# Loading v's weights from a second queue and reordering the first projection of an attention kernel

## The chip, the cores and the metric

The kernel runs on one core of one Trainium2 chip. The metric is the device time of one execution in microseconds. The kernel before takes 255.29 us, the median of three runs (254.67 to 255.47).

## The reference

Two independent blocks, A and B, each take x (2048 tokens, 640 features) and weights, and their outputs are put side by side. Both split 640 features into 32 heads of 20.

```
qkv = x @ wqkv                        # [2048, 3 * 640]: q, k, v
A: scores = q k^T / sqrt(20), each token sees itself and the 255 before it
   o = softmax(scores) v;  out_A = o @ wo
B: pq, pk = phi(q), phi(k)            # phi(t) = t + 1 above zero, exp(t) below
   o = pq (pk^T v) / (pq . sum pk);   out_B = o @ wo
```

The change touches only the first steps of block A: x of the first 512 tokens, v of those tokens (`x @ wqkv`, last third of the columns) and the preparation of q's weights.

## The kernel before

Tokens go in four blocks of 512. Features are five tiles of 128 (KT = 5), so a product over all features is a chain of five matmuls. After an opening written out by hand, the main loop goes through 76 score tiles of block A (`scores`, L784 the products, L792 the exponential, L807 the masks); between them, `take` fills TensorE with projections of A and B from a plan with due times (`chain`, L276, holds most of those products). The change lies in the opening, and the plan is not touched.

The opening, in the order of the program:

- `load_x_first` loads the first 512 tokens of A in rows to a tile (`phi` in the profile) with `load` (L173), as tokens 0 to 127, 128 to 255, and 256 to 511; `transposes` (L178) turns one block of 128 tokens with five transposes into a PSUM tile (`first`), and two copies bring it to `xA`: VectorE's (L352) for even blocks, ScalarE's (L349) for odd ones.
- v's weights come in three parts by feature tile, `v_parts`: tile 0 (160 KB), tiles 1 and 2 (320 KB), tiles 3 and 4 (320 KB), into `wA` (L968). All are issued by SP: tokens 0 to 127, tokens 128 to 255, first part, tokens 256 to 511, second part, third part, then q's and k's raw weights (L334, 800 KB each, into the tiles that the profile calls `qpad` and `kpad`), a transposing load of the next 512 tokens (L163), and B's first weights and x.
- `warm_up` (L196) gives TensorE products of a zeroed tile that nobody reads: 18 before the transposes of the first block of 128 tokens, and 2 between those of the first and the second block.
- `v_abreast` (L411 the products) computes v for the 512 tokens in eight sums: four blocks of 128 tokens times two halves of the columns. The first four sums are in `dense` tiles of PSUM, the last four in `first` tiles. The loop is over parts outside and sums inside: all eight sums take their products of part one, then of part two, then of part three. After the first four products, the caller's loop puts in the transposes of the third and fourth block. The first four sums are evicted (`v_rows`, by `evac`, L261 ScalarE and L263 VectorE) as each ends; after the last product, the caller's loop calls `regroup` for q, and then the last four sums are evicted.
- `regroup` copies the raw weights of q (then of k) into `wqk`, with each head at a 32-row place: for q, five copies of VectorE (L352), and seven that POOL (L355) and ScalarE (L349) take in turn.
- Then come q's rows (three blocks) and k's rows (two) for the first 512 tokens, by `chain` (L276), and the first score tile. A `dense` tile of PSUM is one of four buffers; q's first row takes the one that the first sum of v had.

Of the kernel before, what the change touches and what calls it, by code (L numbers as in the profile page):

```python
# [9 lines left out]
P = 128  # L10
# [4 lines left out]
F32 = mybir.dt.float32  # L15
# [5 lines left out]
SB = 512  # L21
TPS = SB // P
# [70 lines left out]
def kernel(  # L93
# [10 lines left out]
    nc = tc.nc  # L104
    _, S, D = A_x.shape
    KT = D // P
# [31 lines left out]
    first_ps = opening.enter_context(tc.tile_pool(name="first", bufs=4, space=PSUM))  # L138


    w_sb = {}
# [19 lines left out]
    def load_x(n, s):  # L161
        t = xp.tile([P, KT, SB], BF16, name=f"x{n}")
        nc.sync.dma_start_transpose(out=t[:], in_=xsrc[n][s * SB : (s + 1) * SB, :])  # L163
        return t

    def load_x_first():

        tok = pqp.tile([P, TPS, D], BF16, name="phi")
        src = xsrc["A"][0:SB, :].rearrange("(t p) d -> p t d", p=P)
        t = xp.tile([P, KT, SB], BF16, name="xA")  # L170

        def load(t0, t1):
            nc.sync.dma_start(out=tok[:, t0:t1, :], in_=src[:, t0:t1, :])  # L173

        def transposes(tb):
            ps = first_ps.tile([P, 2 * SB], BF16, name="first")
            for c in range(KT):
                nc.tensor.transpose(  # L178
                    ps[:, c * P : (c + 1) * P], tok[:, tb, c * P : (c + 1) * P], ident[:]
                )  # L180
            dst = t[:, :, tb * P : (tb + 1) * P]
            pv = ps[:, 0:D].rearrange("p (c q) -> p c q", q=P)

            for c in (slice(0, 2), slice(2, KT)):
                (act_copy if tb % 2 else dve_copy)(dst[:, c, :], pv[:, c, :])

        return t, load, transposes

    def warm_up(wait):

        z = op.tile([P, TPS, D], BF16, name="osb")
        nc.vector.memset(z[:, 0, 0:P], 0.0)
        ps = dps.tile([P, SB], F32, name="dense")
        for n in wait:
            for _ in range(n):
                nc.tensor.matmul(  # L196
                    ps[:, 0:P], lhsT=z[:, 0, 0:P], rhs=z[:, 0, 0:P], start=True, stop=True
                )
            yield


# [25 lines left out]
    def flush(before=None):  # L227

        while later and (before is None or later[0][0] <= before):
            later.pop(0)[1]()  # L230
# [9 lines left out]
    def settle(all=True):  # L240
        while posts and (all or posts[0][0] <= begun[0]):
            posts.pop(0)[1]()


    load = {"A": 0, "D": 0}
# [9 lines left out]
    def evac(dst, src, n=SB, to=None):  # L255

        if to is None:
            to = "A" if load["A"] < load["D"] + AHEAD else "D"
        load[to] += n + COPY
        if to == "A":  # L260
            nc.scalar.activation(out=dst, in_=src, func=ACT.Copy)  # L261
        else:
            nc.vector.tensor_copy(out=dst, in_=src)  # L263

    def bank(wide=False):
        flush(begun[0] - 2)
        begun[0] += 1
        settle(False)
        if wide:
            return dps.tile([P, 2 * SB], BF16, name="dense")  # L270
        return dps.tile([P, SB], F32, name="dense")
# [40 lines left out]
    xA, xB = {}, {}  # L312
    q_pad, k_pad, v_tok = {}, {}, {}
# [7 lines left out]
    for c in range(KT):  # L321
        m = EXTRA * c
        while m < EXTRA * (c + 1):
            n = min(EXTRA * (c + 1) - m, DH - m % DH)
# [3 lines left out]
    def load_raw(i):  # L328

        pl, name = ((qp, "qpad"), (kp, "kpad"))[i]  # L330
        t = pl.tile([P, NG, SB], BF16, name=name)
        raw = t.rearrange("p g q -> p (g q)")[:, 0 : KT * D].rearrange("p (k n) -> p k n", n=D)
        wv = A_wqkv.rearrange("(kt p) n -> p kt n", p=P)
        nc.sync.dma_start(out=raw, in_=wv[:, :, i * D : (i + 1) * D])  # L334
        return raw

    def regroup(i, src, heads, extras):

        def four(g):
            return src[:, :, 4 * DH * g : 4 * DH * (g + 1)].rearrange("p k (j d) -> p k j d", d=DH)  # L340

        for c in range(KT):
            dst = wqk[:, i, :, c * P : (c + 1) * P].rearrange("p k (j e) -> p k j e", e=32)
            heads(dst[:, :, :, 0:DH], four(c))
            for _, row, g, d, n in [piece for piece in pieces if piece[0] == c]:
                extras(dst[:, :, :, row : row + n], four(g)[:, :, :, d : d + n])

    def act_copy(dst, src):
        nc.scalar.activation(out=dst, in_=src, func=ACT.Copy)  # L349
# [7 lines left out]
    def in_turn(*fns):  # L357
        n = [0]

        def copy(dst, src):  # L360
            n[0] += 1
            fns[n[0] % len(fns)](dst, src)

        return copy
# [43 lines left out]
    by_tokens = [(tb, i) for tb in range(TPS) for i in range(2)]  # L408

    def v_product(ps, xt, tb, i, kt):  # L410
        nc.tensor.matmul(  # L411
            ps[:, 0 : hh * DH],
            lhsT=xt[:, kt, tb * P : (tb + 1) * P],
            rhs=w_sb["A"][:, kt, i * hh * DH : (i + 1) * hh * DH],
            start=(kt == 0),
            stop=(kt == KT - 1),
        )

    def v_rows(ps, dst, tb, i):
        evac(  # L420
            dst[:, tb, i * hh : (i + 1) * hh, 0:DH],
            ps[:, 0 : hh * DH].rearrange("p (h d) -> p h d", d=DH),
            hh * DH,
        )
# [8 lines left out]
            v_rows(ps, dst, tb, i)  # L433
            yield End(hh * DH)

    def v_abreast(xt, dst, order, parts):

        own = len(order) - 4
        pss = {c: bank() for c in order[:own]}
        for k0, k1 in parts:  # L440
            for c in order:
                if c not in pss:
                    pss[c] = first_ps.tile([P, SB], F32, name="first")
                for kt in range(k0, k1):
                    v_product(pss[c], xt, *c, kt)
                if k1 == KT and c in order[:own]:
                    v_rows(pss[c], dst, *c)
                elif k0 == 0:
                    yield
        yield  # L450
        for c in order[own:]:
            v_rows(pss[c], dst, *c)


# [505 lines left out]

    v_parts = ((0, 1), (1, 3), (3, KT))
    wv = A_wqkv.rearrange("(kt p) n -> p kt n", p=P)
    load_tokens(0, 1)
    load_tokens(1, 2)
    for k0, k1 in v_parts:
        if k0 == 1:
            load_tokens(2, TPS)
        nc.sync.dma_start(out=w_sb["A"][:, k0:k1, :], in_=wv[:, k0:k1, 2 * D : 3 * D])  # L968
    raw = [load_raw(i) for i in range(2)]
    xA[1] = load_x("A", 1)  # L970
    load_w("B", B_wqkv, 1, nc.sync)
    xB[0] = load_x("B", 0)
    dummies = warm_up((18, 2))
    for tb in range(2):
        next(dummies)
        transposes(tb)
    v_tok[0] = v_bufs[0]
    for i, _ in enumerate(v_abreast(xA[0], v_tok[0], by_tokens, v_parts)):
        if i == 3:
            transposes(2)  # L980
            transposes(3)
        elif i == 8:
            regroup(0, raw[0], dve_copy, in_turn(act_copy, pool_copy))
    regroup(1, raw[1], in_turn(dve_copy, act_copy), in_turn(act_copy, pool_copy))
    opening.close()
    sps = pool("sps", 1, PSUM)
# [122 lines left out]
    for i, (s, parts, selects, done) in enumerate(units):  # L1109
# [7 lines left out]
        if ready and ready[0][0] + LAG <= i:  # L1117
# [3 lines left out]
            _, at = ready.popleft()  # L1121
# [10 lines left out]
    while ready:  # L1132
        take(5500)
        _, at = ready.popleft()
# [36 lines left out]
```

## Time and profile before

| what | value |
|---|---|
| median of three runs | 255.29 us (254.67 to 255.47) |
| the profiled execution | 255.21 us |
| its span in the trace | 253.5 us |
| TensorE busy | 242.4 us, 96% of the span |
| VectorE, ScalarE, POOL busy | 169.5, 196.8, 186.3 us |
| granted TensorE clock | 1.00 |
| TensorE busy from 0 to 18 us | 15.86 us |
| first product of v, last product of v ends | 4.25 us, 12.73 us |
| first score product | 18.06 us |

PE is TensorE's matmuls, PEld its weight loads, DVE VectorE, ACT ScalarE, POOL GpSimd, and SPq the queue from which SP issues transfers. A row such as `PE dense L411` is a matmul of line 411 that writes a tile named `dense`; `x8` is the number of instructions merged. Times are microseconds from the start of the span. In the timeline, what stands in square brackets is the engine's idle time before the instruction and what ended it. The chain is followed back from the last instruction of the kernel, at each step to what released it.

### The profile page before, as it was taken

To read this page: it belongs to the slowest core of one execution; us is meant where nothing else is said; L and a number is where in the kernel's file an instruction comes from. 1 tells how busy PE (TensorE), PEld (TensorE's weight loads), DVE (VectorE), ACT (ScalarE), POOL (GpSimd) and SP (SyncE) were. 2 spreads that over 40 slices of the span, in tenths; PEclk is the share of its full clock that TensorE was granted. 3 is DMA by queue.
4 is the path that set the end of the run, shared out by engine and by line. 5 is a ranking of instruction groups with operands and counts; after the bars stand their busy time and mean duration, and the time that the engine had idled before them with its cause. 6 is when DMAs were issued, how large, how long until landed. Compare 5 with 4: busy or idle time off the path is not lost.

```text
span 253.5 us, 8721 instructions
## 1 busy us (share of the span) xinstructions
PE 242.4 (96%) x3677; PEld 141.2 (56%) x3723; DVE 169.5 (67%) x311; ACT 196.8 (78%) x194; POOL 186.3 (73%) x310
## 2 busy tenths in 40 slices
PE   7999999999999999999999999999999999999994
PEld 5644446556755546457445555556455465655573
DVE  1264777767754565767664867677889779859662
ACT  3366788898767788997657888889988899999541
POOL 1125798878787798687778969889877978999800
PEclk9999999999999999999999999999999999999999
DMA  6997699897764252994559495525969956494614
GB/s 195 329 263 152 113 188 109 104 288 192 98 119 28 44 193 41 226 291 127 88 106 185 110 199 117 140 34 86 186 104 171 182 89 168 93 181 101 193 58 153
DMA packets 68396, 37.04 MB, mean 146 GB/s; under 512 B 51589, under 2 KB 67333, under 8 KB 68357
## 3 DMA queue, kind: packets, MB, share of 16 engines
q1 hardware_dynamic: 68357, 36.49, 68.5%
q8 instruction: 29, 0.48, 0.7%
q14 instruction: 10, 0.08, 0.1%
HBM read 14.42 MB, written 9.83 MB: 96 GB/s over the span
## 4 chain that ended last, share of the span: by engine, by line
PE 80%; ACT 6%; issue 5%; DVE 4%; DMA 2%; POOL 1%; SPq 0%; ACTq 0%
PE dense L276 46%; PE S_ps L784 10%; PE dense L559 8%; PE dense L831 7%; PE dense L411 5%; ACT p L792 4%; DMA phi<-in_A_x_dram 2%; ACT e L286 1%; DVE phi L293 1%; PE first L411 1%; POOL p L807 1%; PE dense L713 1%; DVE e L290 1%; DVE tok L749 1%; PE dense L642 1%
## 5 line engine op out<-in xcount | busy, mean ns | idle before, releaser
L807 POOL TENSOR_SCALAR_AFFINE_SELECT p<-p 128x256 bf16<-128x256 bf16 (+2 forms) x280 | 176.5, 660 | 43.3 <-ACT p L792 41.8
L792 ACT ACTIVATE p<-S_ps 128x2048 bf16<-128x2048 f32 x76 | 142.9, 1880 | 33.6 <-PE S_ps L784 29.4
L276 PE MATMUL dense<-xA,wqk 128*128 128x512 bf16 x188 | 48.9, 380 | 1.4 <-issue 1.0
L784 PEld LDWEIGHTS <-kpad 20*128 20x128 bf16 (+1 forms) x1216 | 21.9, 98 | 29.5 <-issue 25.5
L784 PE MATMUL S_ps<-qpad,kpad 20*65 20x64 bf16 (+3 forms) x1216 | 33.7, 227 | 0.3
L844 DVE STREAM_TRANSPOSE T<-dense 128x512 f32<-128x512 f32 x32 | 22.8, 713 | 15.7 <-PE dense L831 15.3
L290 DVE TENSOR_SCALAR e<-e 128x512 bf16<-128x512 bf16 x40 | 18.4, 459 | 20.5 <-ACT e L286 20.5
L293 DVE SCALAR_TENSOR_TENSOR phi<-dense,e 128x512 bf16<-128x512 f32 x40 | 27.7, 692 | 1.6
L276 PEld LDWEIGHTS <-wqk 128*128 128x128 bf16 x200 | 17.9, 98 | 19.2
L831 PE MATMUL dense<-p,vA 128*32 128x64 bf16 (+2 forms) x1216 | 25.9, 231 | 0.6 <-ACT osb L261 0.4
L276 PE MATMUL dense<-wB,xB 128*128 128x128 bf16 (+1 forms) x155 | 25.3, 297 | 0.5 <-issue 0.3
L276 PE MATMUL dense<-xB,wB 128*128 128x512 bf16 x90 | 24.6, 380 | 0.6 <-issue 0.3
L276 PE MATMUL dense<-wo,oT 128*128 128x512 bf16 (+4 forms) x161 | 24.5, 293 | 0.6 <-DVE phi L293 0.3
L559 PE MATMUL dense<-tok,phi 128*128 128x129 bf16 (+1 forms) x152 | 24.1, 296 | 0.9 <-issue 0.8
L286 ACT ACTIVATE e<-dense 128x512 bf16<-128x512 f32 x40 | 23.6, 600 | 1.4 <-PE dense L276 0.8
L411 PE MATMUL dense<-wA,xA 128*128 128x320 bf16 x140 | 24.0, 304 | 0.2 <-issue 0.2
L276 PE MATMUL dense<-wB,xA 128*128 128x128 bf16 (+1 forms) x153 | 22.9, 296 | 0.6 <-issue 0.5
L831 PEld LDWEIGHTS <-vA 128*32 128x32 bf16 x1216 | 19.4, 97 | 4.2 <-issue 1.3
L261 ACT ACTIVATE osb<-dense 128x512 bf16<-128x512 f32 (+2 forms) x28 | 15.8, 578 | 5.7 <-PE dense L276 5.5
L411 PEld LDWEIGHTS <-xA 128*128 128x128 bf16 x160 | 14.9, 98 | 8.5 <-ACT xA L349 0.8
L749 DVE TENSOR_TENSOR tok<-tok,rden 128x640 bf16<-128x640 bf16 x16 | 18.3, 1141 | 0.2 <-issue 0.2
L861 DVE TENSOR_TENSOR N<-T,recA 128x320 bf16<-128x320 f32 (+1 forms) x28 | 16.1, 574 | 3.4 <-DMA oT<-N 2.5
(66 smaller groups left out, 196.8 us busy)
## 6 DMA issues: line engine op xcount, KB each, us to landing
out_dram<-osb SPq DMA_DIRECT2D x7, 640.0 KB
x_scr<-xB SPq DMA_DIRECT2D x4, 640.0 KB
tok<-in_B_x_dram SPq DMA_DIRECT2D x4, 640.0 KB
xB<-x_scr SPq DMA_DIRECT2D x4, 640.0 KB
wB<-in_B_wqkv_dram SPq DMA_DIRECT2D x3, 800.0 KB
q_scr<-qpad SPq DMA_DIRECT2D x16, 60.0 KB
k_scr<-kpad SPq DMA_DIRECT2D x16, 60.0 KB
qpad<-q_scr SPq DMA_DIRECT2D x16, 60.0 KB
```

Source lines behind the costliest of these rows:

```text
L276: nc.tensor.matmul(dst, lhsT=lhs(kt), rhs=rhs(kt), start=(kt == 0), stop=(kt == KT - 1))
L286: nc.scalar.activation(out=view(e), in_=src, func=ACT.Exp)
L290: nc.vector.tensor_scalar(out=e[:], in0=e[:], scalar1=1e-6, scalar2=1.0 + 1e-6, op0=ALU.add, op1=ALU.min)
L293: nc.vector.scalar_tensor_tensor(out=dst, in0=src, scalar=0.0, in1=view(e), op0=ALU.max, op1=ALU.add)
L411: nc.tensor.matmul(ps[:, 0 : hh * DH], lhsT=xt[:, kt, tb * P : (tb + 1) * P], rhs=w_sb["A"][:, kt, i * hh * DH : (i + 1) * hh * DH], start ...
L559: nc.tensor.matmul(out, lhsT=pk[:, tb, c * P : (c + 1) * P], rhs=x[:, tb, lo:hi], start=(i == 0), stop=(i == len(blocks) - 1),)
L749: nc.vector.tensor_tensor(out=vh, in0=vh, in1=rden_of[s][:, tb, :, :].to_broadcast([P, H, DH]), op=ALU.mult)
L784: nc.tensor.matmul(S_ps[0:keys, j, col : col + n], lhsT=k_pad[kb // TPS][rows, g, ko : ko + keys], rhs=q_pad[s][rows, g, q0 : q0 + n], sta ...
L792: nc.scalar.activation(out=p, in_=S_ps[:], func=ACT.Exp, scale=scale)
L807: nc.gpsimd.affine_select(out=dst, in_=v, pattern=[[0, 4], [0, n], [sgn, w]], compare_op=ALU.is_ge, fill=0.0, base=base, channel_multiplie ...
L831: nc.tensor.matmul(O_ps[32 * j : 32 * (j + 1), q0 : q0 + n], lhsT=v_flat[kb // TPS % 3][:, at + j * HV : at + j * HV + 32], rhs=p[:, j, co ...
L844: nc.vector.transpose(out=T.rearrange("p b e -> p (b e)"), in_=O_ps[:])
```

## The change

- The three parts of v's weights are no longer all issued by SP. SP issues the first part; the second and third are issued by ScalarE.
- `warm_up` zeroes two tiles: the first 128 columns of feature tile 1 in v's weight tile, and the old one. The first nine products read the former, so ScalarE's first load, which writes there, waits for them; nine more and the last two read the latter. A one-column copy by ScalarE stands ahead of its loads.
- `v_abreast` has another order: first-part products of the first four sums; transposes of the third and fourth block; second-part products of the first four sums; first- and second-part products of the last four; third-part products of all eight. Then `regroup` for q, then all eight evictions.

```diff
     def warm_up(wait):
         z = op.tile([P, TPS, D], BF16, name="osb")
-        nc.vector.memset(z[:, 0, 0:P], 0.0)
+        zeros = [w_sb["A"][:, v_parts[1][0], 0:P], z[:, 0, 0:P]]
+        for t in zeros:
+            nc.vector.memset(t, 0.0)
+        act_copy(z[:, 1, 0:1], z[:, 0, 0:1])
         ps = dps.tile([P, SB], F32, name="dense")
-        for n in wait:
+        for i, n in enumerate(wait):
+            t = zeros[min(i, 1)]
             for _ in range(n):
-                nc.tensor.matmul(
-                    ps[:, 0:P], lhsT=z[:, 0, 0:P], rhs=z[:, 0, 0:P], start=True, stop=True
-                )
+                nc.tensor.matmul(ps[:, 0:P], lhsT=t, rhs=t, start=True, stop=True)
             yield
...
-    def v_abreast(xt, dst, order, parts):
-        own = len(order) - 4
-        pss = {c: bank() for c in order[:own]}
-        for k0, k1 in parts:
-            for c in order:
+    def v_abreast(xt, dst, order, parts, turn, between):
+        pss = {}
+
+        def products(cs, part):
+            for c in cs:
                 if c not in pss:
-                    pss[c] = first_ps.tile([P, SB], F32, name="first")
-                for kt in range(k0, k1):
+                    pss[c] = bank() if c in order[:4] else first_ps.tile([P, SB], F32, name="first")
+                for kt in range(*part):
                     v_product(pss[c], xt, *c, kt)
-                if k1 == KT and c in order[:own]:
-                    v_rows(pss[c], dst, *c)
-                elif k0 == 0:
-                    yield
-        yield
-        for c in order[own:]:
+
+        products(order[:4], parts[0])
+        turn()
+        products(order[:4], parts[1])
+        products(order[4:], (0, parts[1][1]))
+        products(order, parts[2])
+        between()
+        for c in order:
             v_rows(pss[c], dst, *c)
...
-    load_tokens(0, 1)
-    load_tokens(1, 2)
-    for k0, k1 in v_parts:
-        if k0 == 1:
-            load_tokens(2, TPS)
-        nc.sync.dma_start(out=w_sb["A"][:, k0:k1, :], in_=wv[:, k0:k1, 2 * D : 3 * D])
+    def load_v(part, eng):
+        k0, k1 = part
+        eng.dma_start(out=w_sb["A"][:, k0:k1, :], in_=wv[:, k0:k1, 2 * D : 3 * D])
+
+    dummies = warm_up((9, 9, 2))
+    next(dummies)
+    next(dummies)
+    load_tokens(0, 1, nc.sync)
+    load_tokens(1, 2, nc.sync)
+    load_v(v_parts[0], nc.sync)
+    load_tokens(2, TPS, nc.sync)
+    load_v(v_parts[1], nc.scalar)
+    load_v(v_parts[2], nc.scalar)
     raw = [load_raw(i) for i in range(2)]
...
-    dummies = warm_up((18, 2))
-    for tb in range(2):
-        next(dummies)
-        transposes(tb)
+    transposes(0)
+    next(dummies)
+    transposes(1)
     v_tok[0] = v_bufs[0]
-    for i, _ in enumerate(v_abreast(xA[0], v_tok[0], by_tokens, v_parts)):
-        if i == 3:
-            transposes(2)
-            transposes(3)
-        elif i == 8:
-            regroup(0, raw[0], dve_copy, in_turn(act_copy, pool_copy))
+    v_abreast(
+        xA[0],
+        v_tok[0],
+        by_tokens,
+        v_parts,
+        lambda: (transposes(2), transposes(3)),
+        lambda: regroup(0, raw[0], dve_copy, in_turn(act_copy, pool_copy)),
+    )
```

More of the change, by code (lines that the diff above doesn't have):

```diff
@@ L170, in load_x_first, with load @@
         t = xp.tile([P, KT, SB], BF16, name="xA")
-        def load(t0, t1):
-            nc.sync.dma_start(out=tok[:, t0:t1, :], in_=src[:, t0:t1, :])
+        def load(t0, t1, eng):
+            eng.dma_start(out=tok[:, t0:t1, :], in_=src[:, t0:t1, :])
         def transposes(tb):
```

## The prediction

> **What bounds the kernel now.** I read the page first, then the chain of waits that ended last over the first 14 us, then the timelines of SP's queue, ScalarE and VectorE over the same stretch.
>
> ```profile
> span 253.5 us, 8721 instructions
> PE 242.4 (96%) x3677; PEld 141.2 (56%) x3723; DVE 169.5 (67%) x311; ACT 196.8 (78%) x194; POOL 186.3 (73%) x310
> PE 80%; ACT 6%; issue 5%; DVE 4%; DMA 2%; POOL 1%; SPq 0%; ACTq 0%
> ```
>
> TensorE is busy for 96% of the span and carries 80% of the chain; DMA has 2%, about 5 us, and the next answer shows that nearly all of it is one wait in the opening, the only part that the change touches. From about 13 us on, the work follows TensorE instruction by instruction, so a microsecond that TensorE loses or gains in the opening should arrive at the end nearly whole. The opening's chain:
>
> ```profile
> 2.19 4.26 DMA phi<-in_A_x_dram
> 6.45 0.05 issue
> 6.50 0.75 PE first L178 x10
> 7.25 0.02 issue
> 7.27 0.77 ACT xA L349 x2
> 8.04 0.04 issue
> 8.08 0.30 PE first L411
> 8.38 1.09 PE dense L411 x8
> 9.47 1.09 PE first L411 x8
> 10.55 1.09 PE dense L411 x8
> 11.64 1.09 PE first L411 x8
> 12.73 0.22 PE dense L276
> ```
>
> Columns are start, length and what. Two things stand ahead of v's products: the transfer of tokens 256 to 511 (I call it the **last tokens**), issued at 2.19 and whole at 6.45, and, after the ten transposes, ScalarE's two copies out of PSUM, 7.27 to 8.04. From 8.38 to 12.73 TensorE runs without a gap, 32 products in 4.35 us, 0.136 us each. Then q's rows (L276) begin, so 12.73 is the figure to move.
>
> The issues, from SP's timeline, and ScalarE's:
>
> ```profile
> 2.19 0.43 SPq L173 DMA_DIRECT2D phi<-in_A_x_dram  x1
> 2.66 0.98 SPq L968 DMA_DIRECT2D wA<-in_A_wqkv_dram  x2
> 3.69 0.47 SPq L334 DMA_DIRECT2D qpad<-in_A_wqkv_dram  x1
> ```
>
> ```profile
> 0.80 1.28 ACT L349 ACT_TABLE_LOAD   x1 [0.80 <-PEq L1155]
> 4.49 0.77 ACT L349 ACTIVATE xA<-first 128x256 bf16<-128x256 bf16 x2 [2.40 <-PE first L178]
> ```
>
> The trace also records the sixteen completions of each transfer. The last tokens complete between 5.00 and 6.45, v's second part between 5.85 and 7.28, the third between 6.79 and 8.11, q's raw weights between 9.47 and 10.36, k's by 12.58. The last ones of the three 320 KB transfers are 0.83 us apart: that is the price of one such transfer in front of another.
>
> **The change, part by part.**
>
> *Second-part products over the copies.* After the transposes, 36 products are left (4 + 32). Before, only the four first-part products of tokens 256 to 511 stand beside the copies: from 7.25 to 8.38 TensorE has 1.13 us for 4 x 0.136 = 0.54 us of work. After, the eight second-part products of tokens 0 to 255 stand there: 8 x 0.136 = 1.09 us from 7.25 to 8.34, longer than the copies (8.04), so the wait is covered. The 36 products then run without a gap: 7.25 + 36 x 0.136 = 12.15, against 12.73: **0.58 us less**. If v's second part lands no earlier than before, at 7.28, the first of these products starts at 7.33, as the first one does now, and the gain is 0.50. I take 0.55. No product is added or left out.
>
> *v's parts from ScalarE's queue.* No transfer is issued there in this trace. The first issue waits for the table load (ends 2.08), the small copy (the nearest rows are copies of 0.33 to 0.49 us) and the nine products that read the zeroed weights. The 18 warm-up products take 2.10 us from 1.06, so the ninth ends at about 2.2. The issue begins at about 2.4, 0.26 us ahead of the 2.66 at which SP issues it now. Each issue costs between nothing and 7.97 us (the transposing issue behind full queues, SP's longest); I take SP's rows for such a transfer, 0.47 each, because the shape is the same and the queue is empty. ScalarE is then free at 3.35 and its next work comes at 4.49: hidden, with 1.1 us to spare. Without that cover, the copies of tokens 128 to 255 would be late, and TensorE, which idles from about 5.6 to 6.5 anyway, would absorb 0.9 us more. At the top end, ScalarE would be held until about 10.3 or beyond and the kernel would lose 3 to 4 us; nothing near that row applies, and I leave it outside the range.
>
> SP issues two transfers fewer, 1.03 us: q's goes from 3.69 to 2.66, k's from 4.20 to 3.17, the transposing load of x from 4.77 to 3.74. The data, not the issues, set when these land (from 5.5 to 11 us the queues move 340 to 390 GB/s), so I give them nothing. The later loads that they hold up (x and B's weights) are not on the chain.
>
> What this does to the last tokens is the open term. They stay fourth on SP's queue, but v's second part no longer stands behind them, it runs beside them, and q's weights follow on SP. Below: the tokens' completions are spread over 1.45 us where q's are spread over 0.89, so 0.56 us could go. Above: 0.83 us for each of v's two parts that overtakes them. From 3.5 to 4.5 us the queues move only 141 and 164 GB/s by the windows of the trace, against 379 at 5.5 to 6, so about (379 - 152) x 1 us = 227 KB, two thirds of a part, could move in a stretch that now stands half empty. I take no change at 6.45, between the ends and nearest to the present row, because the idle stretch pays for most of one overtaking.
>
> The Trainium skill (DMA: Bandwidth & Descriptors, "Queues, rings and completion order") says that each DMA engine goes round between the queues it has work for, a packet of several descriptors at a time. By that rule alone, v's second part would share from about 3.4 us on and the tokens would end near 7.28; no run here has two busy queues yet, and it speaks against the change. It is the second rival below.
>
> *The extra zeros.* One memset (0.11 us, VectorE, which is idle until 3.74) and no product more: 9 + 9 + 2 instead of 18 + 2. Nothing.
>
> *q's regroup ahead of v's sums.* The same 12 copies and 8 evictions, in another order. POOL starts at 10.41 now, when q's weights land. VectorE's five copies (1.01 us) and ScalarE's three (0.84) could then run from 10.41: q's first block is ready by about 10.7, for 12.18. But the evictions now stand behind: the first ends at 10.41 + 0.84 + 0.44 = 11.69, and q's first row takes that PSUM buffer at 12.18. It has 0.5 us to spare, so the cost is nothing; if q's weights land after 10.85, each microsecond later is lost. ScalarE's backlog up to k's regroup is the same work begun 0.45 us earlier, so k's blocks are not late either.
>
> *Sum.* 0.55 us on the path, the rest hidden: 255.21 (this execution: 253.5 span and 1.7 around it) - 0.55 = **254.7**. The median of the runs shown, 255.29, is 0.08 above this execution, which changes nothing that I can tell. A difference within 0.3%, 0.77 us, is about what a measurement of this kernel can tell from none; the forecast lies just inside that bound.
>
> **The rivals.**
>
> 1. *The tokens come earlier.* If the last of sixteen completions comes 0.89 us after the first, as q's do, they are whole at 5.9 and the products end at 11.6; the first eviction at 11.69 then sets q's rows at about 11.75. Gain 1.0: **254.2**. For it: the spread of 1.45 comes with long stalls in the half-empty stretch. Against: nothing that the change does removes a stall.
>
> 2. *Sharing eats the gain.* v's second part alternates with the tokens and both end at 7.28. Then 7.28 + 0.05 + 0.75 + 4.90 = 12.98 against 12.73: 0.25 lost, **255.5**. For it: both are then issued within 0.3 us of each other. Against: the half-empty stretch. This is the outcome of the skill's rule.
>
> 3. *Both parts overtake (slower).* If ScalarE's queue is drained first, the tokens wait for 640 KB and end at 8.11, where v's third part ends now: 8.11 + 5.70 = 13.81, 1.08 lost, **256.3**. It is slower than 0.3% from the point at which the tokens land after 7.8. For it: the first part's issue comes at 2.4, when the tokens' issue is not yet over. Against: the second issue, near 2.9, comes well after theirs.
>
> 4. *q comes late.* With v's parts beside it rather than ahead, q's weights could end with k's, at 12.58. The evictions and q's rows then wait: 12.58 + 1.33 = 13.9, 1.2 lost, **256.4**. Against: q would have to share with k, which is behind it in its own queue.
>
> **How the numbers follow.** The forecast has 0.43 (0.19 of it beyond 0.3% faster, since its own range is 254.3 to 255.0, and the measurement adds some 0.2), rival 1 0.21, rival 2 0.19, rival 3 0.13, rival 4 0.04. So faster 0.19 + 0.21 = 0.40, the same 0.24 + 0.19 = 0.43, slower 0.13 + 0.04 = 0.17. The range reaches from just under rival 1, 254.0, over rival 2 to 256.0, and leaves out rivals 3 and 4 in the main. Faster and same, next to each other, hold most of the chance.
>
> **What would show it.** In the profile after: two issues of wA on ScalarE's queue at 2.4 to 3.4; eight products on dense behind the transposes with no gap; the last token at 6.3 to 6.6 (rival 1: 5.9, rival 2: 7.3, rival 3: 8.1); q's first row (L276 of before) at about 12.2; POOL's first regroup copy still near 10.4; and the same 0.5 us still there at the first scores, 18.06 in this trace. I am wrong if the tokens' landing moves by more than 0.3 us, if the products find v's second part missing, or if the shift is there at 18 us but not at the end.

## The result and the profile after

The changed kernel takes 257.05 us, the median of 21 runs (254.54 to 259.26), against 254.87 us for the kernel before (254.41 to 255.92): a ratio of 1.0074, 95% interval 1.0053 to 1.0095. It is slower, by some 0.7% and clear of the noise, where 0.55 us less was forecast. The ratio leaves out the three slowest runs of the changed kernel (258.44 to 259.26); the quotient of the two medians is 1.0086. The profiled execution took 257.05 us, with a span of 255.3.

The page of the changed kernel, its first lines and the granted clock in 40 slices:

```profile
span 255.3 us, 8721 instructions
PE 243.2 (95%) x3677; PEld 141.8 (56%) x3723; DVE 168.8 (66%) x312; ACT 197.2 (77%) x195; POOL 186.4 (73%) x310
PEclk9799999999999999999999999999999999999999
```

TensorE's work is the same (3677 matmuls; VectorE and ScalarE have one small instruction more each); what stands out is the 7 in the second slice of the clock. The chain of waits over the opening (start, length, what):

```profile
2.19 5.12 DMA phi<-in_A_x_dram
7.31 0.05 issue
7.36 1.03 PE first L178 x10
8.39 2.13 PE dense L415 x8
10.52 1.95 PE first L415 x12
12.47 1.09 PE dense L415 x8
13.56 1.09 PE first L415 x8
14.65 0.22 PE dense L280
```

The last tokens are whole at 7.31, not 6.45. The wait for the copies is gone, as the change meant. But the first eight products take 2.13 us where eight took 1.09, and twelve take 1.95 where 12 x 0.136 = 1.63. Time by stretches, TensorE alone (length, busy time and count, granted clock, DMA share, GB/s):

```profile
0.81:4.22 3.41, 3.12 (x27) 1.00 0.64 158
4.22:7.64 3.42, 1.36 (x14) 1.00 1.00 335
7.64:11.05 3.41, 3.41 (x20) 0.50 1.07 369
11.05:14.46 3.41, 3.41 (x27) 1.00 1.28 231
```

I laid these stretches by the trace's clock record, which changes at 4.222, 7.635 and 11.049, each 3.413 us behind the one before. In the second TensorE is busy for 1.36 of 3.42 us; in the third it has half its clock.

The account of the 1.92 us from 12.73 (before) to 14.65 closes: tokens later 0.86; ten transposes 1.03 instead of 0.75, 0.28; eight products 2.13 instead of 1.09, 1.04; twelve products 1.95 instead of 1.63, 0.32; the copies' wait, no longer there, -0.58. So the half clock adds 1.64, the later landing 0.86, and the new order takes 0.58 off. The first score product comes at 19.98 instead of 18.06, again 1.92, and the span ends 1.8 later.

Where TensorE idled, from the timeline of the changed kernel:

```profile
2.24 0.97 ACTq L972 DMA_DIRECT2D wA<-in_A_wqkv_dram  x2
...
5.49 0.70 PE L415 MATMUL dense<-wA,xA 128*128 128x320 bf16 x4 [0.89 <-DMA wA<-in_A_wqkv_dram]
...
7.36 1.03 PE L178 MATMUL first<-ident,phi 128*128 128x128 bf16 x10 [1.16 <-DMA phi<-in_A_x_dram]
```

ScalarE's two issues start at 2.24. The first part of v's weights, still on SP's queue, is whole at 5.45 (4.18 before), so v's first product waits 0.89 us; then the transposes wait 1.16.

### The profile page after: what moved, and what is told of

Its sections match the earlier page's. It is cut to its first block, busy times and chain, and to the rows that moved or that the text cites. A ratio compares the mean times of both kernels' runs of the same rounds, so it can differ in the third digit from the quotient of the medians.

```text
span 255.3 us, 8721 instructions
## 1 busy us (share of the span) xinstructions
PE 243.2 (95%) x3677; PEld 141.8 (56%) x3723; DVE 168.8 (66%) x312; ACT 197.2 (77%) x195; POOL 186.4 (73%) x310
## 4 chain that ended last, share of the span: by engine, by line
PE 84%; issue 4%; ACT 4%; DVE 4%; DMA 2%; SPq 0%; POOL 0%; ACTq 0%
PE dense L280 46%; PE S_ps L791 10%; PE dense L566 8%; PE dense L838 8%; PE dense L415 7%; ACT p L799 2%; DMA phi<-in_A_x_dram 2%; PE first L415 1%; DVE phi L297 1%; ACT e L290 1%; PE dense L720 1%; DVE e L294 1%; DVE tok L756 1%; PE dense L649 1%; PE dense L677 1%
## 5 line engine op out<-in xcount | busy, mean ns | idle before, releaser
L415 PEld LDWEIGHTS <-xA 128*128 128x128 bf16 x160 | 15.7, 101 | 9.2 <-issue 1.0
L280 PEld LDWEIGHTS <-oT 128*128 128x128 bf16 x165 | 13.2, 98 | 8.4 <-issue 0.7
```

Source lines behind the costliest of these rows:

```text
L280: nc.tensor.matmul(dst, lhsT=lhs(kt), rhs=rhs(kt), start=(kt == 0), stop=(kt == KT - 1))
L415: nc.tensor.matmul(ps[:, 0 : hh * DH], lhsT=xt[:, kt, tb * P : (tb + 1) * P], rhs=w_sb["A"][:, kt, i * hh * DH : (i + 1) * hh * DH], start ...
```

## The experiments

**Theory clock:** the later landings leave TensorE idle; for that it is granted half its clock for a stretch of 3.4 us. **Theory landings:** the later transfers cost the time by themselves. **Third theory:** the new order of products or regroup is at fault. Medians are of all runs of a kernel; the kernel before ran on the same chips at 255.03 to 255.22. Unread products are matmuls that nobody reads. Those ahead of the transposes come from one small function, those ahead of v's first product are more of `warm_up`'s:

```diff
+    def spare(n):
+        ps = first_ps.tile([P, SB], F32, name="first")
+        for _ in range(n):
+            nc.tensor.matmul(ps[:, 0:P], lhsT=ident[:], rhs=ident[:], start=True, stop=True)
```

**1. The changed kernel with both waits filled.**

```diff
-    dummies = warm_up((9, 9, 2))
+    dummies = warm_up((9, 9, 2, 8))
...
-        lambda: (transposes(2), transposes(3)),
+        lambda: (spare(12), transposes(2), transposes(3)),
```

The eight stand ahead of v's first product.

> The changed kernel with 20 more unread products: 8 ahead of v's first product, 12 ahead of the transposes of tokens 256 to 511, both in places where TensorE waits for a transfer. Theory clock (the idle TensorE is granted half its clock for a stretch of 3.4 us, which costs about 1.7): the half-clock stretch is gone, and the time is 254.9 to 255.4, though the transfers land as late as in the changed kernel. Theory landings (the later transfers themselves cost the 2.2 us): it stays at 256.5 to 257.5.

255.29 us, ratio to before 1.0002 (0.9983 to 1.0021). Its chain over the opening:

```profile
2.19 5.01 DMA phi<-in_A_x_dram
7.20 0.05 issue
7.25 0.73 PE first L178 x10
7.98 1.09 PE dense L420 x8
9.07 1.63 PE first L420 x12
10.70 1.09 PE dense L420 x8
11.78 1.09 PE first L420 x8
12.87 1.29 PE dense L285 x6
```

The tokens are as late as in the changed kernel (7.20), yet the products run at full clock and the loss is gone. Twenty products that nobody reads take some 1.8 us off the changed kernel. The theory that the landings alone do it falls.

**2 and 3. The two halves of the change alone.** Number 2 has the changed kernel's loads and `warm_up` with the old `v_abreast` and its loop; number 3 has the old loads, all by SP, and `warm_up((18, 2))` with the new `v_abreast` and regroup; its difference to the changed kernel in the loads:

```diff
-    load_v(v_parts[1], nc.scalar)
-    load_v(v_parts[2], nc.scalar)
+    nc.sync.dma_start(out=w_sb["A"][:, k0:k1, :], in_=wv[:, k0:k1, 2 * D : 3 * D])
```

> The queue part alone: v's later parts from ScalarE's queue behind nine products, with the order of v's products and of q's regroup of the kernel before. Theory clock: the two waits are the same, so the half-clock stretch comes here too, 256.5 to 257.5. Theory landings: the last tokens 0.86 later, 255.7. A third theory, that the new order of the products or of the regroup is at fault: 254.9, like before.

256.98 us, 1.0068 (1.0044 to 1.0092). The loss comes with the queue, without the new order; by stretches of its trace:

```profile
6.04:9.45 3.41, 1.68 (x15) 1.00 1.05 369
9.45:12.87 3.42, 3.42 (x15) 0.50 1.22 260
```

Again a stretch that is half idle, then one at half clock; tokens at 7.55.

> The order alone: the new order of v's products and q's regroup ahead of v's sums, with all parts on SP's queue and 18 + 2 warm-up products as before. Theories clock and landings: the transfers land as before, the clock stays, and the gain of the prediction, 0.5 to 0.6, shows: 254.3. Third theory (the order is at fault): 256 to 257.

255.45 us, 1.0013 (0.9993 to 1.0034): no loss, so the third theory falls, but no gain either, against what I expected. Its trace shows tokens early (6.06) and no gap after them, but six of the eight products behind the transposes at half clock: full clock came only at 8.82, where the profile of the kernel before had it at 6.09.

**4. The kernel before with its own wait filled.** `spare(8)` ahead of `transposes(2)` in the old loop.

> The kernel before with 8 unread products ahead of the transposes of tokens 256 to 511, in its one wait of 0.9 us. Theories clock and landings: the kernel before has no half-clock stretch to lose after 6 us, so 254.9, the same as before; if its slower runs (up to 255.9) have one, these go.

255.07 us, 0.9989 (0.9967 to 1.0011): nothing to gain there, as expected.

**5. The order alone, wait filled.** Number 3 with `spare(10)` ahead of `transposes(2)`.

> The order alone (loads on SP as before) with 10 unread products ahead of the transposes of tokens 256 to 511. Theory clock: the order alone gained nothing because TensorE came to its full clock only at 8.8 us; with the wait filled it comes there by 7, the products run without a gap at full clock, and the gain of 0.5 shows: 254.6 against 255.1 of the kernel before on the same chip. Theory that the order costs something by itself: it stays at 255.2 to 255.5, like the order alone.

254.78 us, 0.9981 (0.9961 to 1.0001). In its profile the eight products behind the transposes are at full clock (299 ns each; this trace has no clock record), and the first score comes at 17.49, 0.57 ahead of before and 0.92 ahead of number 3. In number 3's profile the transposes take 1.07 us instead of 0.75 and the eight products 1.82 instead of 1.09, 1.05 us in all: the gain that number 3 lacked went to the clock. The interval of number 5 just includes no gain.

**6. The kernel before with 3 warm-up products instead of 18.**

> The kernel before with 3 warm-up products in place of 18; no transfer, no order and nothing read is changed. Theory clock: TensorE is idle from about 1.4 to 3, stays at half its clock until after 8 us, and the kernel takes 256.3 to 257.5, as long as the changed one, though all transfers land as before. Theory landings: 255.1, the same as before, since the 15 products are read by nobody and stand beside transfers.

255.72 us, 1.0007 (0.9983 to 1.0031): a miss in size. The direction is there in the profile (full clock at 9.30, products 426 to 474 ns long instead of 299 until then, the first score at 18.78, 0.72 later, with tokens at 6.21), but the medians are only 0.55 us apart, the ratio gives 0.2, and its interval includes none. In its chain the wait for the copies is gone: the slow products cover it, which hides part of their price. All ten runs have a mean granted clock of 1.000, so a late rise does not show in that figure: the trace's record begins with the first full clock.

**7. ScalarE's issues behind 18 products.** Number 1 with `warm_up((18, 0, 2, 8))`.

> The changed kernel with the 20 more unread products, and ScalarE's issues behind 18 unread products in place of 9, so at about 3.1 us in place of 2.24. If the order of issue decides who lands first, the last tokens land near 6.5 again (7.2 with nine) and v's second part near 7.5; the time is then 254.5 to 254.8. If the two queues share whatever the issue, the tokens stay near 7.1 and the time at 255.2.

258.94 us, 1.0132 (1.0086 to 1.0178). The first half of the expectation came true, tokens whole at 6.08; the second did not. Who waited, in its trace (total us, times, longest):

```profile
PE dense L420 <- DMA wA<-in_A_wqkv_dram: 2.5, 1, 2.5
```

SP had issued q's weights by 3.14, before ScalarE's first issue at 3.19, and v's second part landed at 10.18 instead of 7.58, together with q's (10.42). So the gate only chooses who is late: with nine products the tokens share with v's second part, with 18 that part shares with q's weights. This wait lost the clock too: the stretch from 6.29 to 9.71 was busy for 0.42 of it, and the next one has half clock, so the 258.94 holds both.

**8. Number 1 with q's regroup back.** The first four sums evicted as each ends, then the regroup.

> The changed kernel with the 20 more unread products, and q's regroup back behind the first four evictions, as before the change. If the regroup's place costs or gains nothing, as predicted, 255.2 to 255.4 as with the 20 products alone; if its place made the changed kernel slower, below 254.8.

255.48 us, 1.0001 (0.9980 to 1.0022), beside 1.0002 with the regroup ahead: its place costs nothing.

**9. The queue alone, waits filled.** Number 2 with the 8 and 12 products.

> The queue part alone, in the old order, with the same 20 more unread products (8 and 12) that brought the whole change back to the time of before. It prices the landings by themselves, at full clock: the last tokens at 7.2 in place of 6.45 move the first score by 0.75, and the order does not give 0.55 back, so about 255.9 against 255.2 of the kernel before; by the rule that a stretch of 3.4 us with TensorE busy for over 0.8 of it leaves the clock full, no half-clock stretch. If the landings cost nothing once the clock is full, 255.2.

256.22 us, 1.0045 (1.0026 to 1.0064), 0.3 above the expectation. No half-clock stretch, and tokens at 8.64 in the profiled run:

```profile
5.94:9.36 3.42, 1.82 (x26) 1.00 1.05 367
9.36:12.77 3.41, 3.23 (x24) 1.00 1.61 293
```

TensorE busy for 1.82 of 3.42 and the clock stays, where 1.68 in number 2 lost it. So at full clock the landings alone cost some 1.1 us in the old order.

**10. The order alone, 4 and 6 unread products** (`warm_up((18, 2, 4))`, the 4 ahead of v's first product, and `spare(6)`).

> The order alone with fewer unread products in two places: 4 ahead of v's first product, 6 ahead of the transposes of tokens 256 to 511 (10 in the second place held the transposes back by 0.4 in the run before: tokens whole at 6.0, transposes at 6.47). If the rest of the gain is there, 254.4 to 254.6 against 255.2 of before; if 6 are too few to keep the stretch busy, some runs at 255.5 and above.

254.83 us, 0.9977 (0.9957 to 0.9997): faster than the kernel before, by 0.32 us between the medians and 0.6 by the ratio, where the prediction wanted 0.55 from the order.

**11 and 12. One wait filled at a time**, in the changed kernel.

> The changed kernel with only the 12 unread products ahead of the transposes. Theory clock: they fill most of the longer of the two waits, so that a stretch laid as in the profile of the changed kernel (4.2 to 7.6) goes from 0.40 busy to about 0.7; where the rule's border lies between 0.49 (dropped) and 0.81 (kept) decides it: 255.3 if 0.7 is enough, 256 to 257 in some runs if not.

> The changed kernel with only the 8 unread products ahead of v's first product. The wait for the last tokens stays open (1.2 to 1.4 us with the copies' wait ahead of it), so a stretch from about 6 to 9.4 is still busy for only half: 256.3 to 257, most of the loss remains. If the first wait is what drops the clock, 255.3.

Number 11: 256.30 us, 1.0049 (1.0021 to 1.0076), spread from 254.96 to 259.30. In its profile the clock rose only at 10.10, because the stretch from 3.27 to 6.69, with the open first wait, was busy for just 0.70 of its length; tokens at 8.32. Number 12: 255.81 us, 1.0038 (1.0006 to 1.0069), lower than I expected, and in two groups: seven runs at 255.13 to 255.89 with a mean granted clock of 0.998 or more, five at 257.06 to 259.29 with 0.985 to 0.993. One half-clock stretch lowers the mean by 0.5 x 3.41 / 250 = 0.007, so the second group is the dropped clock (the 0.985 twice), and it costs about 2 us.

Neither wait is harmless. With the second one open (number 12) the clock drops in five of twelve runs, but no run without a drop is over 255.89. With the first one open (number 11) it drops in three of twelve (0.986 to 0.993), and runs without a drop go up to 257.87; that one is the profiled run with the late rise, which costs it 0.8 us (transposes 1.25 instead of 0.75, the eight products 1.39 instead of 1.09). So the first wait delayed the rise there. Whether the other long runs without a drop are late rises too is not shown: no trace of them was kept.

**13 to 16. Four more profiled runs of the changed kernel,** one execution each, since its one profile could not tell whether all runs lose in this way.

> The changed kernel again, one look. If the clock is behind all its loss, a time above 256 goes with v's products at 0.27 us each (474 ns long) for 2 us or more after the transposes of tokens 256 to 511, from a late rise (first full clock at 9 to 11 us) or a drop; a time below 255 goes with products at 0.136 throughout. If the landings alone do it, a time above 256 comes with full-clock products and tokens whole at 8.5 or later.

> The same as the look before it: slow products with a time above 256 (clock), or full-clock products and tokens at 8.5 or later (landings).

> The same as the two looks before it: slow products with a time above 256 (clock), or full-clock products and tokens at 8.5 or later (landings).

> The same as the three looks before it: slow products with a time above 256 (clock), or full-clock products and tokens at 8.5 or later (landings).

257.92, 255.31, 256.32 and 255.54 us. The first two by stretches:

```profile
5.04:8.45 3.41, 0.70 (x4) 1.00 1.04 358
8.45:11.86 3.41, 3.39 (x19) 0.50 1.26 358
```

```profile
5.06:8.47 3.41, 1.75 (x18) 1.00 1.05 370
8.47:11.88 3.41, 3.41 (x27) 1.00 1.21 350
```

Tokens at 8.43 in the first and at 7.37 in the second: 0.70 us busy, and the clock drops; 1.75 us, and it stays. The run at 255.54 (tokens at 7.11) is like the second. The one at 256.32 fits neither theory: full clock from 5.67, tokens at 7.22, first score at 18.22. From the first to the 21st exponential of the scores it takes 57.50 us, as number 11's profile does, and the other sixteen profiles 56.67 to 56.97; from the first score to the end of the span it takes 236.4 us. Number 11 and the run at 255.54 have 236.0 and 235.7 there, all others 235.1 to 235.4. So three of the twelve profiles with two queues, and none of the six with one, lose 0.3 to 1.3 us far behind the opening. The cause is open, and so is whether the change has a part in it.

Not every run loses by a dropped clock, then. Of the 21 timed runs of the changed kernel five have a mean granted clock of 0.993 (256.75 to 257.93), which is one half-clock stretch; the other sixteen, at 0.998 or 1.000, spread from 254.54 to 259.26. For these, the clock's part is not seen; it is inferred from number 1, where the time of before comes back once the waits are filled.

## Why the prediction was wrong

The number, 254.7, and the range, 254.0 to 256.0, were both missed. By its own steps:

- **The last tokens, "I take no change at 6.45": this step failed.** With one queue the tokens were whole at 6.00 to 6.45 (six profiles: before and numbers 3, 4, 5, 6, 10); with parts issued from ScalarE's queue at 2.24, at 7.11 to 8.64 (eleven profiles; in the changed kernel's, 7.31). No overlap: 0.7 to 2.6 us. My reason for none was that the half-empty stretch from 3.5 to 4.5 would take the extra transfer. It didn't: from 3 to 5 us the changed kernel moved 197 and 206 GB/s, the kernel before 224 and 232.
- **Rival 2 had the landing almost exactly** (7.28; measured 7.31, and v's second part beside it at 7.58), and with it the rule of the Trainium skill that it cited (DMA: Bandwidth & Descriptors, "Queues, rings and completion order"): two busy queues take turns, and the trace agrees: in all eleven profiles the tokens and v's second part end 0.18 to 0.33 us apart. Its time, 255.5, was 1.6 short. Where the clock held it was near: the changed kernel's profiled runs without a drop have 255.31, 255.54 and, with the loss far behind the opening, 256.32. Rivals 3 and 4 had times nearer to the measured one, 256.3 and 256.4, but neither happened: v's third part landed at 10.40, behind the tokens, and q's weights at 10.71, well before k's at 12.96.
- **The missing term: the clock.** The sum let idle TensorE time cost nothing ("would absorb 0.9 us more"), without a reason, and no rival had it. A stretch busy for 0.40 of its length cost 1.64 us in the profile. That TensorE can be at half clock could have been read from the trace of before, from groups of equal products (from 3.9 to 6.6 us, and from 10 to 13):

```profile
L411 PE MATMUL dense<-wA,xA 128*128 128x320 bf16 x4 | 1.4, 466 | 0.0
L411 PE MATMUL dense<-wA,xA 128*128 128x320 bf16 x8 | 1.2, 299 | 0.0
```

Behind the bar stand the busy us and the mean ns of one. V's first products are 449 to 474 ns long, the later ones 299; and five transposes take 0.71 us at 2.99 and ten 0.75 at 6.50, so TensorE was at half clock until its record begins, at 6.09. The page's row of nines doesn't show it, since nothing is recorded before that.
- **The first part of v's weights,** which the change left on SP's queue, I took as untouched. It landed at 5.45 instead of 4.18 in the profiles, and its wait, 0.89 us, is nearly half of the idle time. This may not be the change's doing: it varies from 4.20 to 5.61 with two queues and from 4.18 to 5.12 with one.
- **The products over the copies were right.** From tokens whole to q's first row the kernel before takes 12.73 - 6.45 = 6.28 us and number 1, at full clock, 12.87 - 7.20 = 5.67: 0.61 less (forecast 0.55). It shows in the time only where the clock is full (numbers 5 and 10, 0.3 to 0.4 us by the medians; number 5's interval includes none).
- **ScalarE's issues, the zeros, the regroup were right:** issues from 2.24 to 3.21 (forecast 2.4 to 3.35), 0.45 and 0.48 each; number 8 for the regroup; q's weights reached POOL at 10.77 instead of 10.41, which TensorE didn't feel. The reading beside it, 340 to 390 GB/s from 5.5 to 11 us, was loose: from 6.5 to 7.5 the trace has 312 and 284.
- **That the shift arrives whole was right:** from first score to the end of the span, before has 235.4 us, the changed kernel 235.3, and numbers 1 to 10 between 235.1 and 235.3; number 11 and two of the four further profiles (256.32 and 255.54 us) are the exceptions.

What stays open is why the tokens vary from 7.11 to 8.64 with two queues, where the long runs without a dropped clock lose their time, and the loss far behind the opening.

## What to carry to other kernels

Before a transfer is moved to a second queue, look at what lands while it runs: here the two queues shared one bandwidth, and a transfer that was safely in front had company. Where TensorE waits in an opening, its wait can have a second price, the clock of the next microseconds; read it from the length of equal matmuls, not from the page's clock row alone. And measure an edit that fills a gap together with what keeps the clock up, or its gain may not show.

## What the runs showed of the hardware

- The granted clock changes on a grid of 3.413 us, whose place differs from run to run (first entries at 4.22 to 10.10 us), and follows how busy TensorE was in the stretch before. Busy shares worked out from seventeen traces (union of the matmuls, on each trace's own grid):

| share of the stretch that TensorE was busy | clock then |
|---|---|
| 0.21, 0.40, 0.42, 0.49 | falls from full to half |
| 0.51, 0.53, 0.57, 0.63, 0.67, 0.81, 0.83 | stays full |
| up to 0.82 (0.65, 0.70, 0.70, 0.78, 0.82) | stays at half |
| 0.85 to 1.00 | rises to full |

In these traces, then, it falls at about half busy (between 0.49 and 0.51) and rises only above some 0.83 (between 0.82 and 0.85). The Trainium skill (TensorE: Matmul & The Clock Gate, "Part 1: The HAM clock gate") gives the free-running window of 3413 ns, which the traces agree with. Its advice under "Why this matters for your kernels", no idle gaps over about 3 us, does not suffice here: in the opening of the changed kernel's profile no gap between matmuls is longer than 1.2 us, and the stretch with two of them lost the clock.
- A transfer issued 0.95 us later on a second queue (3.19 instead of 2.24) landed 2.6 us later (10.18 instead of 7.58), with q's 800 KB issued on the first queue in between, at 2.67. One trace shows this; why the step is so large is not shown.
